# Weighted sums in 64-row halves of the array, projections in bursts, relu on two engines and squares on three

## The chip, the cores and the metric

The kernel runs on one core of one Trainium2 chip. A core has five engines that work side by side, each with its own queue of instructions in a fixed order: TensorE (PE in the profile; its weight loads are shown apart as PEld), VectorE (DVE), ScalarE (ACT), GpSimd (POOL) and SyncE (SP), which here only issues transfers. TensorE writes its results to a small memory, PSUM, in eight banks; VectorE and ScalarE read them there and write to the large on-chip memory. The metric is the device time of one execution, in microseconds (us).

## The reference

Two operators follow one another. The first is a gated attention without softmax, the second a gate with a long convolution along the sequence. For 8 batches, a sequence of S = 3136 and a width of D = 256 (`z` has a width of 64):

```
scores = z @ z.T / S                       # 3136 x 3136, per batch
attn   = maximum(scores, 0) ** 2
x      = u * (attn @ v)                    # 3136 x 256
x1, x2, x3 = split(x @ w_proj, 3)          # w_proj is 256 x 768
conv   = irfft(rfft(x2, axis=seq) * filter_fft, axis=seq)
out    = (x1 * conv * x3) @ w_out
```

The matrix `scores` is symmetric, so is `attn`.

## The kernel before

**Tiling.** A batch's columns of `attn` are cut into seven chunks (`CHUNKS`: five of 512, one of 256, one of 320), its rows into 25 tiles of 128, of which the last holds 64. For one chunk the kernel goes over the row tiles, two at a time (four in the 256-wide chunk); such a pair is a unit.
- *Scores* (`score_mm`, kind "S"): two matmuls with 64 rows of weights, because `z` is 64 wide. They lie in the upper and in the lower half of the array and run at the same time. Their two results fill a pair of PSUM banks; there are three such pairs (`ps_t`).
- *Relu* (line 1852) by ScalarE from PSUM to the buffer `R` in float32 (three of them), *square* (lines 1859 and 1861) by ScalarE or VectorE from `R` to `A` in bfloat16 (eight of them).
- *Weighted sum* (`weigh`, kind "W"): for each row tile and each of the two halves `dh` of the width one matmul with 128 rows, `v` as weights and `A` as the moving operand. All of a chunk add up in two PSUM banks, `ps_o[0]` and `ps_o[1]`. Some units, kind "M", need no scores: they take the transposed copy of a tile that was squared for an earlier chunk. The odd 64 rows at the end are added by `weigh_short`.
- *End of a chunk* (line 1903): VectorE multiplies the two finished banks with `u` and writes `x` (`xT`), two instructions for each bank; then the banks are free for the next chunk.
- *Projections and the convolution* (kinds "FA", "FB", "FZ", all with 128 rows): `x` times `w_proj`, the first and last steps of the Fourier transform, and the product with `w_out`. Their results go through single banks of the three pairs and leave by ScalarE or VectorE. The middle steps of the transform (`add_quads`, kind "Q") use quarters of the array, 64 rows by 64 columns.

**Shapes of the array.** So TensorE works in two shapes: with 128 rows (sums, projections) and with 64 rows (scores, quads; with 64 columns too while a quad is near, `plan.quarters`). All matmuls are issued by the helper at line 561, so the profile gives this line for all and tells them apart by tiles (`ps_s`, `ps_o_t`, `zT_t`, `v_t`).

**Order of the work.** Nothing loops on the chip: the class `Plan` writes out the order of every queue beforehand. It keeps a clock per engine, with a cost for each kind of work (`c_act`, `c_dve`, `c_pe`), and picks the next task of TensorE (`pick_pe`) and of the other engines (`pick`). A change between the two shapes is charged 0.096. While scores can start (a free pair of banks), they go on; else the plan turns to sums and projections. A table, `RULES`, gives the parameters of these choices for each 50 us of the plan's clock. Projections are let in by a credit: each sum adds `pace`, each projection takes its cost off; the credit goes no higher than 2.0. The plan only sets the order. On the chip each engine takes its queue in that order, and semaphores make it wait for what it needs.

**At the ends of a chunk** `add_weigh` puts the sums of the first and the last units for `dh = 1` off (`put_off`), so that the two banks begin and end at different times.

**Buffers and queues.** GpSimd issues the loads of `u`, `v` and `z` two chunks ahead; each such step begins with a copy of one element (`tick`, line 644), which waits for the chunk's `x`. SyncE issues the other transfers.

Of the kernel before, what the change touches and what calls it, by code (L numbers as in the profile page):

```python
# [12 lines left out]
P = 128  # L13
# [4 lines left out]
ALU = mybir.AluOpType  # L18
# [19 lines left out]
MOST = 3  # L38
REACH = 2
Rule = namedtuple("Rule", "backlog ample stay first lead pace full give")  # L40
STEP = 50.0
RULES = [
    Rule(1.25, 5.0, 0.05, 0.5, 1, 0.5, 3.0, 1.0),
    Rule(1.25, 5.0, 0.05, 0.5, 1, 0.5, 3.0, 1.0),
    Rule(1.25, 5.0, 0.05, 0.5, 1, 0.45, 3.0, 1.0),
    Rule(1.25, 5.0, 0.05, 0.5, 1, 0.45, 3.0, 1.0),
    Rule(1.25, 5.0, 0.05, 0.5, 1, 0.45, 3.0, 1.0),
    Rule(1.25, 5.0, 0.05, 0.5, 1, 0.5, 3.0, 1.0),
    Rule(1.25, 5.0, 0.05, 0, 1, 0.55, 3.0, 1.0),
    Rule(1.25, 5.0, 0.05, 0.5, 1, 0.5, 3.0, 1.0),  # L50
    Rule(1.25, 5.0, 0.05, 0.5, 1, 0.5, 3.0, 1.0),
    Rule(1.25, 6.0, 0.05, 0.5, 1, 0.5, 3.0, 1.0),
    Rule(1.25, 6.0, 0.05, 0.5, 1, 0.5, 3.0, 1.0),
    Rule(1.25, 5.0, 0.05, 0.5, 1, 0.5, 3.0, 1.0),
    Rule(0.5, 6.0, 0.05, 0, 0, 0.4, 99, 0.5),
    Rule(0.5, 6.0, 0.05, 0, 0, 0.4, 99, 0.5),
    Rule(0.5, 6.0, 0.05, 0, 0, 0.4, 99, 0.5),
    Rule(1.25, 5.0, 0.1, 1, 1, 0.5, 3.5, 1.0),
    Rule(1.75, 99.0, 0.3, 0.5, 1, 0.55, 4.0, 1.0),
    Rule(1.25, 5.0, 0.05, 0.5, 1, 0.5, 3.0, 0),  # L60
    Rule(1.25, 5.0, 0.3, 0.5, 1, 0.6, 3.0, 1.0),
    Rule(1.25, 5.0, 0.05, 0.5, 1, 0.5, 3.0, 0),
# [14 lines left out]
def c_dve2(n):  # L77
    return 0.068 + n * 0.00052

# [103 lines left out]
class Task:  # L183


    def __init__(self, emit, cost, deps=(), takes=(), prio=0, lat=None, moves=0.0, late=0.0):
# [6 lines left out]
        self.end = None  # L193
        self.holders = 1
# [11 lines left out]
class Plan:  # L206


    def __init__(self):
# [7 lines left out]
        self.soon = False  # L217
        self.n = 0
        self.spare = []
        self.pairs = None  # L220
        self.bus = 0.0

# [30 lines left out]
    def run(self, task, engine, start):  # L253
# [6 lines left out]
        task.end = end  # L260
        task.emit(engine)
# [36 lines left out]

    def pick_pe(self):
        t = self.free["PE"]  # L300
        now = self.rule(t)
        got = {}
        for k, window in (("S", 1), ("Q", 4), ("W", 1), ("FA", 6), ("FB", 6), ("FZ", 6)):
            best = None
            for task in self.queues[k][:window]:
                s = max(t, self.ready_at(task))
                if s < INF and (best is None or s < best[0] - 1e-9):
                    best = (s, task)
            if best:
                got[k] = best  # L310
        if not got:
            return None
        more = self.queues["S"]
        quad = got.pop("Q", None)
        if self.mode == "S" and self.quarters and quad and quad[0] <= t + now.stay:
            if not more or self.quad_run < 1 and self.score_run >= now.lead:
                return (*quad, "Q")
        if more and not more[0].left:
            left = self.backlog()
            if self.mode == "S":  # L320
                if "S" in got and got["S"][0] <= t + now.stay:
                    return (*got["S"], "S")
                got.pop("S", None)
                if self.quarters and quad and quad[0] <= t + now.stay and self.quad_run < 1:
                    return (*quad, "Q")
            else:
                want = 3 if left > now.ample else 2
                free = self.pairs.when(min(want, len(more)) - 1)
                first = quad and quad[0] <= t + 0.3 and left > now.first
                if "S" in got and free > t + 0.04:  # L330
                    rest = {k: v for k, v in got.items() if k != "S" and (k == "W" or left > now.backlog)}
# [1665 lines left out]
```

## Time and profile before

| | |
|---|---|
| median of 3 runs | 986.96 us (986.27 to 987.56) |
| span of the profiled execution, first to last instruction | 983.6 us |
| TensorE busy | 946.7 us (96%), 6,776 matmuls |
| weight loads busy | 470.0 us (48%), 6,877 |
| VectorE busy | 832.4 us (85%) |
| ScalarE busy | 855.6 us (87%) |
| GpSimd busy | 204.4 us (21%) |
| granted TensorE clock, mean | 0.998 |

The page has no other time of the profiled execution than its span; what an execution takes before the first and after the last instruction is in the runs' times and not in it. How to read the rows: a row of a group names the line, the engine, the operation, what is written and read (tile names without buffer numbers), the shape, and after "x" the count; behind the bar stand the busy time in us, the mean duration of one in ns, and the idle time of the engine just before them with what ended it. "64\*128 64x512" is a matmul with 64 rows and 128 columns of weights and 512 columns of the moving operand. The busy time of TensorE is a union of matmul durations; as matmuls are pipelined, the distance from one start to the next tells more than a duration.

### The profile page before, as it was taken

To read this page: it belongs to the slowest core of one execution; us is meant where nothing else is said; L and a number is where in the kernel's file an instruction comes from. 1 tells how busy PE (TensorE), PEld (TensorE's weight loads), DVE (VectorE), ACT (ScalarE), POOL (GpSimd) and SP (SyncE) were. 2 spreads that over 40 slices of the span, in tenths; PEclk is the share of its full clock that TensorE was granted. 3 is DMA by queue.
4 is the path that set the end of the run, shared out by engine and by line. 5 is a ranking of instruction groups with operands and counts; after the bars stand their busy time and mean duration, and the time that the engine had idled before them with its cause. 6 is when DMAs were issued, how large, how long until landed. Compare 5 with 4: busy or idle time off the path is not lost.

```text
span 983.6 us, 19551 instructions
## 1 busy us (share of the span) xinstructions
PE 946.7 (96%) x6776; PEld 470.0 (48%) x6877; DVE 832.4 (85%) x1468; ACT 855.6 (87%) x1185; POOL 204.4 (21%) x426
## 2 busy tenths in 40 slices
PE   6999999999999999999999999999999999999986
PEld 2344544455544544445444454544544454544654
DVE  8966798998788887988879998799788997888885
ACT  5988898899888998899988899799988999999773
POOL 5142311222022301213111230113202222000040
PEclk9999999999999999999999999999999999999999
DMA  9799789979899689997699888997869978896677
GB/s 166 140 175 160 144 144 172 180 131 162 179 216 187 128 159 203 192 184 144 143 210 197 167 153 175 209 192 151 157 158 205 215 137 146 178 221 135 172 209 227
DMA packets 332403, 170.32 MB, mean 173 GB/s; under 512 B 242598, under 2 KB 307942, under 8 KB 332304
## 3 DMA queue, kind: packets, MB, share of 16 engines
q1 hardware_dynamic: 302496, 132.43, 63.1%
q0 software_dynamic: 29168, 35.13, 23.7%
q10 hardware_dynamic: 640, 1.51, 0.5%
q8 instruction: 54, 0.88, 0.4%
q14 instruction: 45, 0.37, 0.1%
HBM read 90.26 MB, written 53.35 MB: 146 GB/s over the span
## 4 chain that ended last, share of the span: by engine, by line
PE 77%; DVE 10%; ACT 5%; issue 5%; DMA 1%; ACTq 0%; POOL 0%; DVEq 0%; SPq 0%; POOLq 0%
PE ps_o_t L561 45%; PE ps_s L561 32%; DVE A_t L1861 4%; ACT R_t L1852 3%; DVE xT_t L1903 1%; DVE xh L1307 1%; DVE gate_t L1217 1%; DVE yT_t L1401 1%; ACT A_t L1859 1%; DMA spec<-s_t 0%; ACT x_t L594 0%; DVE gs_t L598 0%; ACT s_t L594 0%; DMA spec<-gs_t 0%; DMA zn_t<-in_z_dram 0%
## 5 line engine op out<-in xcount | busy, mean ns | idle before, releaser
L1852 ACT ACTIVATE R_t<-ps_s 128x1024 f32<-128x1024 f32 (+4 forms) x512 | 467.0, 965 | 71.2 <-PE ps_s L561 68.0
L561 PE MATMUL ps_o_t<-A_t,v_t 128*128 128x512 bf16 (+4 forms) x2009 | 447.5, 353 | 9.7 <-issue 4.8
L1861 DVE TENSOR_TENSOR A_t<-R_t 128x1024 bf16<-128x1024 f32 (+3 forms) x311 | 342.8, 1119 | 58.9 <-ACT R_t L1852 58.3
L561 PEld LDWEIGHTS <-v_t 128*128 128x128 bf16 (+2 forms) x2870 | 249.0, 98 | 259.8 <-issue 74.5
L1859 ACT ACTIVATE A_t<-R_t 128x1024 bf16<-128x1024 f32 (+4 forms) x185 | 186.5, 1018 | 1.2
L561 PE MATMUL ps_s<-zT_t 64*128 64x512 bf16 (+4 forms) x1512 | 169.9, 357 | 1.6 <-DVE zT_t L598 0.5
L644 POOL COPY tick<-xT_t 1x1 bf16<-1x1 bf16 x54 | 17.9, 331 | 693.7 <-DVE xT_t L1903 693.7
L561 PE MATMUL ps_s<-xT_t,wp 128*128 128x512 bf16 (+2 forms) x412 | 101.1, 351 | 3.6 <-ACT R_t L1852 0.9
L561 PEld LDWEIGHTS <-zT_t 64*64 64x64 bf16 (+1 forms) x1545 | 52.6, 101 | 101.7 <-issue 85.8
L594 ACT ACTIVATE x_t<-ps_s 128x512 bf16<-128x512 f32 (+2 forms) x152 | 82.2, 583 | 16.0 <-PE ps_s L561 12.1
L1903 DVE SCALAR_TENSOR_TENSOR xT_t<-ps_o_t,uT_t 128x256 bf16<-128x256 f32 (+2 forms) x224 | 76.1, 383 | 10.8 <-PE ps_o_t L561 8.6
L1307 DVE TENSOR_TENSOR xh<-xh,H 128x1024 bf16<-128x1024 bf16 x120 | 82.3, 686 | 0.8
L561 PE MATMUL ps_o_t<-M_t,v_t 128*128 128x512 bf16 (+2 forms) x352 | 81.8, 353 | 0.0
L1217 DVE TENSOR_TENSOR gate_t<-ps_s,x_t 128x256 bf16<-128x256 f32 (+2 forms) x214 | 71.0, 384 | 12.5 <-PE ps_s L561 10.7
L1401 DVE TENSOR_TENSOR yT_t<-ps_s,gate_t 128x512 bf16<-128x512 f32 (+2 forms) x98 | 58.4, 626 | 11.1 <-PE ps_s L561 10.1
L561 PEld LDWEIGHTS <-wp 128*128 128x128 bf16 x448 | 42.6, 98 | 45.6 <-issue 10.3
L635 POOL DMA_DIRECT2D un_t<-in_u_dram x112 | 60.1, 561 | 5.3 <-issue 4.5
L654 POOL DMA_DIRECT2D v_t<-in_v_dram x112 | 59.6, 557 | 4.8 <-DMA v_t<-in_v_dram 1.9
L598 DVE CAST xh<-ps_s 128x512 bf16<-128x512 f32 x62 | 41.8, 687 | 18.6 <-PE ps_s L561 17.7
L561 PE MATMUL ps_s<-wp,xT_t 128*128 128x256 bf16 x398 | 56.6, 273 | 0.2
L561 PE MATMUL ps_s<-wo,yT_t 128*128 128x256 bf16 (+1 forms) x338 | 49.8, 273 | 0.7 <-ACT R_t L1852 0.4
L594 ACT ACTIVATE s_t<-ps_s 128x512 bf16<-128x512 f32 (+1 forms) x82 | 46.9, 593 | 1.8 <-issue 0.9
(165 smaller groups left out, 840.9 us busy)
## 6 DMA issues: line engine op xcount, KB each, us to landing
out_dram<-ost_t SPq DMA_DIRECT2D x60, 256.0 KB
spec<-s_t SPq DMA_DIRECT2D x96, 128.0 KB
spec_in_t<-spec SPq DMA_DIRECT2D x56, 192.0 KB
spec<-gs_t SPq DMA_DIRECT2D x56, 192.0 KB
v_t<-in_v_dram POOLq DMA_DIRECT2D x80, 128.0 KB, 4.8
un_t<-in_u_dram POOLq DMA_DIRECT2D x80, 128.0 KB, 5.4
conv_in_t<-spec SPq DMA_DIRECT2D x34, 256.0 KB
out_dram<-ost_t SPq DMA_DIRECT2D x18, 128.0 KB
```

The lines of the kernel that those rows point to most:

```text
L561: wrote(nc.tensor.matmul(o, *args, **kw), o)
L594: got = nc.scalar.activation(out_, in_, AF.Copy)
L598: got = nc.vector.tensor_copy(out_, in_)
L635: nc.gpsimd.dma_start(out=t[ds(j * N1, N1), lo - t0 : hi - t0, :], in_=x[:, n2 : n2 + hi - lo, :])
L654: nc.gpsimd.dma_start(out=t[ds(j * N1, N1), ds(v_at(a), (b - a) * D)], in_=r[:, n2 + a - lo : n2 + b - lo, :].rearrange("p t d -> p (t d)"),)
L1217: got = nc.vector.tensor_tensor(g[:, ::-1] if h == 0 else g, p, x, ALU.mult)
L1307: nc.vector.tensor_tensor(x[:, 1 - i], x[:, 0], h, ALU.mult)
L1401: got = nc.vector.tensor_tensor(yb["y"][:, dh, 0:w], p, gates[b, c, dh][:, 0:w], ALU.mult)
L1852: has_read(nc.scalar.activation(blocks(box["R"], n, cw)[:rows], p, AF.Relu), p)
L1859: nc.scalar.activation(a, r, AF.Square)
L1861: nc.vector.tensor_tensor(a, r, r, ALU.mult)
L1903: nc.vector.scalar_tensor_tensor(x, f, inv_s2, ut, ALU.mult, ALU.mult)
```

## The change

Six things are changed.
1. A unit's weighted sum can be split (`weigh_half`): if the array is in 64-row work when the plan picks it, each 128-row matmul is done as two 64-row ones. In the first phase rows 0 to 63 add into one of the two banks and rows 64 to 127 into the other; the second phase (a task of its own, kind "V", in the list `rest`) does it crosswise. `flip` says which way round. The two row halves must not write the same bank at once: where the rows that add into a bank change, `by_rows` puts an empty instruction on TensorE's queue that waits for the last matmul of the other rows. The plan charges 0.12 for it if nothing lies between.
2. `pick_pe` is written anew. Scores and sums alternate; second phases are gathered up to `many` before the rows are crossed. Projections start when the next sum waits for its banks (or the credit is above `lots`) and go on while there is credit, which may now rise to `cap` (mostly 4.0). All parameters in `RULES` are new.
3. The sums of the first and last units of a chunk aren't put off any more.
4. Relu may run on ScalarE or VectorE.
5. The square may run on ScalarE, VectorE or GpSimd. The plan lets VectorE's squares, VectorE's products with the filter and GpSimd's squares follow one another and not overlap (`ports`), and gives GpSimd one only where it would be done sooner there than on both others.
6. Single banks: up to six may be in use at once (`MOST`, before three). Two loads of the last batch wait for the transform of the batch before (`after_q`).

```diff
-MOST = 3
+MOST = 6
...
+def c_pool(n):
+    return 0.25 + n * 0.0021
...
     def pick_pe(self):
...
+        runs = [k for k in ("S", "Q") if k in got and got[k][0] <= t + now.stay]
...
+        if self.rest:
+            if self.apart or self.flip in (None, self.rest[0].flip):
+                return max(t, self.ready_at(self.rest[0])), self.rest[0], "V"
+            if w and len(self.rest) < now.many:
+                return (*w, "W")
+            if runs:
+                return (*got[runs[0]], runs[0])
+            later = min(((*got[x], x) for x in ("S", "Q") if x in got), key=lambda x: x[0], default=None)
+            if later and later[0] <= t + now.hold:
+                return later
+            return max(t, self.ready_at(self.rest[0])), self.rest[0], "V"
+        kinds = ("FB", "FA", "FZ")
+        fs = [k for k in kinds if k in got and got[k][0] <= near]
+        if self.phase:
+            if fs and (self.credit > 0 or blocked or not self.queues["S"]):
+                return (*got[fs[0]], fs[0])
...
+            self.phase = False
+        if (blocked or self.credit > now.lots) and (fs or self.owed(t)):
...
+            if fs:
+                self.phase = True
+                return (*got[fs[0]], fs[0])
+        if w and self.score_run >= now.lead:
+            if self.mode != "S" or self.pairs.when() <= t + now.many * w[1].cost["PE"] / 2 + now.hold:
+                return (*w, "W")
+        if runs:
+            return (*got[runs[0]], runs[0])
+        if w:
+            return (*w, "W")
+        order = ["S", "Q", "W", "FA", "FB", "FZ"]
         k = min(got, key=lambda k: (got[k][0], order.index(k)))
         return (*got[k], k)
...
+            if e == "POOL" and others:
+                end = s + task.cost[e] - self.rule(t).slack
+                if any(end >= self.could_end(task, o, s) for o in others):
+                    continue
...
-                half = k in ("S", "Q")
+                half = k in ("S", "Q", "V") or k == "W" and self.mode == "S"
...
+                        if self.flip not in (None, task.flip) and not self.apart:
+                            start += 0.12
...
+                    task.split = half and task.second is not None
+                    if task.split:
+                        task.cost["PE"] /= 2
+                        task.second.flip = task.flip ^ 1
+                        self.rest.append(task.second)
...
+    def by_rows(dh, h, *args, **kw):
+        other, last = row_sums.get(dh, (h, None))
+        if other != h:
+            tc.add_manual_dep(
+                nc.tensor.nop().ins, last.ins.name, mybir.DependencyInfo(needs, reason.DATA),
+                reason="the other rows' sum",
+            )
+        inst = nc.tensor.matmul(*args, **kw)
+        row_sums[dh] = h, inst
...
+    def weigh_half(un, flip, first):
...
+            for h in range(2):
+                dh = h ^ flip
+                at = slice(h * N1, (h + 1) * N1)
...
+                for m in range(0, P, N1 if plan.quarters else P):
+                    p = N1 if plan.quarters else P
+                    by_rows(
+                        dh, h, o[ds(m, p)], row(v16[b], t)[at, ds(dh * P + m, p)], x,
+                        start=k == 0 and i == 0 and first, stop=last and i == len(pair) - 1 and not first,
+                    )
...
-        k, n = un[2], global_k
-        if k in (0, n - 3, n - 2):
-            part((0,))
-            if k in (0, n - 3):
-                put_off.clear()
-            put_off.append(part)
-            return None
-        if k in (1, n - 1):
-            part((0,))
-            for late in put_off:
-                late((1,))
-            return part((1,))
         return part((0, 1))
...
-                has_read(nc.scalar.activation(blocks(box["R"], n, cw)[:rows], p, AF.Relu), p)
+                if e == "ACT":
+                    has_read(nc.scalar.activation(r, p, AF.Relu), p)
+                else:
+                    has_read(nc.vector.tensor_single_scalar(r, p, 0.0, ALU.max), p)
...
-                    nc.vector.tensor_tensor(a, r, r, ALU.mult)
+                    (nc.vector if e == "DVE" else nc.gpsimd).tensor_tensor(a, r, r, ALU.mult)
...
-            r_ = on(
-                "ACT", relu, c_act(n * cw), [(st, -sum(costs[i + 1 :]) - extra)], [R_p.slots], prio=0
+            r_ = job(
+                None, relu, both(n * cw), [(st, -sum(costs[i + 1 :]) - extra)], [R_p.slots], prio=0
             )
-            how = {"DVE": c_dve(n * cw)} if (b, c) == (0, 0) and k > 1 else {"DVE": c_dve(n * cw), "ACT": c_act(n * cw) + 0.039}
+            how = {"ACT": c_act(n * cw) + 0.039, "DVE": c_dve(n * cw), "POOL": c_pool(n * cw)}
             q_ = job(None, sq, how, [r_], [a_p.slots], prio=1)
+            q_.ports = ("DVE", "POOL")
```

Of the new parameters, `many` is 2 in 14 of the 20 rows of `RULES`, 1 in four and 3 in two; `lots`, the credit from which projections start unasked, is 99 in 14, which is never, as `cap` is at most 6; `lead` is 1 in 16 and 2 in four.

235 lines of the change are left out of this document (146 added, 89 removed).

## The prediction

> **What bounds the kernel now.** I read the page first (busy shares, then the chain that ended last), then one window over the middle, then the table of waits, and last the timeline of TensorE around one change of array shape.
>
> ```profile
> span 983.6 us, 19551 instructions
> ...
> PE 946.7 (96%) x6776; PEld 470.0 (48%) x6877; DVE 832.4 (85%) x1468; ACT 855.6 (87%) x1185; POOL 204.4 (21%) x426
> ...
> PE 77%; DVE 10%; ACT 5%; issue 5%; DMA 1%; ACTq 0%; POOL 0%; DVEq 0%; SPq 0%; POOLq 0%
> ...
> 100.00:900.00 800.00, 787.14 (x5616) 389.17 (x5704) 689.11 (x1183) 719.33 (x988) 158.35 (x326) 1.00 0.89 173
> ...
> 400.00:500.00 100.00, 98.78 (x713) 48.66 (x723) 88.72 (x153) 92.32 (x129) 20.55 (x41) 1.00 0.89 164
> ...
> PEld L561 <- issue: 199.8, 559, 1.0
> ACT R_t L1852 <- PE ps_s L561: 68.0, 84, 4.2
> DVE A_t L1861 <- ACT R_t L1852: 58.3, 56, 2.4
> ```
>
> TensorE is busy 787 of the 800 us between 100 and 900 (columns of a window row: length, then PE, PEld, DVE, ACT, POOL, granted clock, DMA share, GB/s), at a granted clock of 1.00, and 77% of the last-ending chain is its own work. ScalarE's longest wait is for TensorE's scores (68.0 us), and VectorE's longest in this loop is for ScalarE's relu (58.3). So TensorE sets the pace, and the other two are close behind: 719.33 + 689.11 of 1,600 us is 88.0% over the middle, and the fullest stretch shown, 400 to 500, has 90.5% ((92.32 + 88.72)/200).
>
> But a busy TensorE isn't a streaming one, and the 559 idle spells of its weight loader that nothing but "issue" explains point at what is lost. The timeline shows one:
>
> ```profile
> 481.66 1.46 PE L561 MATMUL ps_o_t<-A_t,v_t 128*128 128x512 bf16 x6
> ...
> 483.05 0.33 PEld L561 LDWEIGHTS <-zT_t 64*128 64x128 bf16 x6 [0.42 <-issue]
> 483.05 0.82 PE L561 MATMUL ps_s<-zT_t 64*128 64x512 bf16 x6
> 483.55 1.96 ACT L1852 ACTIVATE R_t<-ps_s 128x1024 f32<-128x1024 f32 x2
> ...
> 483.81 1.47 PE L561 MATMUL ps_o_t<-A_t,v_t 128*128 128x512 bf16 x6
> ...
> 5.94 1.03 PE L561 MATMUL ps_s<-zT_t 64*128 64x512 bf16 x4 [0.52 <-DVE zT_t L598]
> ...
> 956.86 0.30 PE L561 MATMUL ps_s<-R_t,zT_t 64*64 64x256 bf16 x4
> ...
> L561 PE MATMUL ps_o_t<-A_t,v_t 128*128 128x512 bf16 x1389 | 357.8, 381 | 9.5 <-issue 4.8 <-DVE A_t L1861 1.3 <-DVE xT_t L1903 0.2
> ...
> L561 PE MATMUL ps_s<-zT_t 64*128 64x512 bf16 x487 | 74.2, 383 | 0.8 <-DVE zT_t L598 0.5
> ...
> L561 PEld LDWEIGHTS <-zT_t 64*128 64x128 bf16 x616 | 22.6, 94 | 53.1 <-issue 43.7 <-DVE xT_t L598 0.8 <-DVE zT_t L598 0.8
> ```
>
> Six 128-row matmuls take 1.46 us with 0.38 for the last alone, so they follow one another every (1.46 - 0.38)/5 = 0.216 us. The six that start at 481.66 should be followed at 481.66 + 6 x 0.216 = 482.96. The scores start at 483.05, 0.09 late. They are six matmuls on 64 rows, which run two at a time: 3 x 0.216 = 0.65, so the next weighted sum could start at 483.70; it starts at 483.81, 0.11 late. One stay in the half array costs 483.81 - 481.66 - 9 x 0.216 = 0.206 us more than the work. Read through the whole timeline, the array changes from 128-row to 64-row work 261 times (the rows at 5.94 and 956.86 are in the first and the last); 2 x 261 = 522 changes make up most of the 559 "issue" spells. **261 x 0.206 = 53.8 us**, 5.5% of the span, is what changes of shape cost now.
>
> **The change part by part.** (a) *Weighted sums in row halves.* While the array is in 64-row work, a task of four 128-row matmuls becomes eight 64-row ones: rows 0 to 63 add into one half of the output, rows 64 to 127 into the other, at once; a second phase crosses them. Two 64-row matmuls pass in the 0.216 us that one 128-row matmul takes (scores above), and two weight loads of 94 ns each fit in it even one after the other, so the streaming time stays as it is. Score, sum, score, sum can follow without a change of shape, and only projections still need the full array.
>
> (b) *Projections in longer bursts.* A burst begins when the head of the sums' queue waits for its output banks, that is once per chunk, and lasts while credit (now capped at 4.0 us) is left. There are 56 chunks (the row below: four products per chunk and one semaphore wait each). The largest projection groups are busy 101.1 + 56.6 + 49.8 = 207.5 us, 3.7 us per chunk, so one burst per chunk can hold them all.
>
> ```profile
> L1903 DVE SCALAR_TENSOR_TENSOR xT_t<-ps_o_t,uT_t 128x256 bf16<-128x256 f32 (+2 forms) x224 | 76.1, 383 | 10.8 <-PE ps_o_t L561 8.6
> ...
> L1903 DVEq EVENT_SEMAPHORE  x56: 21/368/2069, 28.5 to 924.1; - x56
> ...
> L561 PE MATMUL ps_s<-xT_t,wp 128*128 128x512 bf16 (+2 forms) x412 | 101.1, 351 | 3.6 <-ACT R_t L1852 0.9
> ...
> L561 PE MATMUL ps_s<-wp,xT_t 128*128 128x256 bf16 x398 | 56.6, 273 | 0.2
> ...
> L561 PE MATMUL ps_s<-wo,yT_t 128*128 128x256 bf16 (+1 forms) x338 | 49.8, 273 | 0.7 <-ACT R_t L1852 0.4
> ```
>
> The floor is 56 stays, the ceiling 261 as now. Against the floor speaks the last line of the picking rule: when no score, quad or sum is ready, a ready projection is taken wherever it stands. I take one of these per chunk (56 more) and 8 for head and tail: 120 stays, 120 x 0.206 = **24.7 us**. Bounds: 11.5 and 53.8.
>
> (c) *The price of a flip.* Between the phases TensorE must wait until the other rows' last matmul into the same bank is done; this is a new wait on its own work, and everything behind it on its queue waits too. No row shows it. From below it is nothing: work that is put between hides it. From above: a matmul of this form lasts 0.383 us, and the first reader of a score starts 0.12 us after it (483.05 + 0.38 = 483.43 against 483.55), so the next could start 0.383 + 0.12 after the last instead of 0.216: 0.29 us. The nearest row is the change of shape, 0.09. With one score pair (0.216) in between 0.07 is left, with two nothing. The program has about 640 sum tasks (24 row tiles x 2 output halves x 56 chunks = 2,688 matmuls, four or, in the 256-wide chunk, eight to a task), most rules gather two before they flip, and scores number 512 (the relu row below), so there is usually a score for each flip: 320 flips, half of them with one score between, 160 x 0.07 = **11.2 us**. Bounds: 0 and 320 x 0.29 = 93.
>
> (d) *The chunk's end.* So far one output half was finished ahead of the other (the put-off parts), which hid the products that empty it. Now both end together, and the next chunk's sums wait for four products of 0.383 us, 1.5 us. The projection burst of 3.7 us hides it; if none were ready it would cost up to 56 x 1.5 = 86 us, but scores are there as well. Zero taken. A squared tile is held until the second phase, up to two sums (1.7 us) longer, with eight buffers: zero. Up to six instead of three single banks may be held by projections, so a score after a burst may find no free pair for one evacuation: zero taken, up to 0.69 us (a 512-column cast, below) x 56 = 38 from above. The added order on the last batch's loads concerns SyncE, 0% of the chain: zero.
>
> (e) *Relu on two engines, squares on three.*
>
> ```profile
> L1852 ACT ACTIVATE R_t<-ps_s 128x1024 f32<-128x1024 f32 (+4 forms) x512 | 467.0, 965 | 71.2 <-PE ps_s L561 68.0
> ...
> L1852 ACT ACTIVATE R_t<-ps_s 128x1024 f32<-128x1024 f32 x408 | 402.5, 1038 | 62.7 <-PE ps_s L561 59.9 <-DVE A_t L1861 1.2
> ...
> L1861 DVE TENSOR_TENSOR A_t<-R_t 128x1024 bf16<-128x1024 f32 x238 | 287.3, 1220 | 46.8 <-ACT R_t L1852 46.3
> ...
> L1859 ACT ACTIVATE A_t<-R_t 128x1024 bf16<-128x1024 f32 x154 | 164.6, 1080 | 1.0
> ...
> L598 DVE CAST xh<-ps_s 128x512 bf16<-128x512 f32 x62 | 41.8, 687 | 18.6 <-PE ps_s L561 17.7
> ...
> L644 POOL COPY tick<-xT_t 1x1 bf16<-1x1 bf16 x54 | 17.9, 331 | 693.7 <-DVE xT_t L1903 693.7
> ```
>
> A relu on VectorE has no row; a cast of half its size takes 0.687, so it lies between 1.22 (VectorE's square of that size) and 1.37, against 1.04 on ScalarE: swaps, no saving. A square on GpSimd has no row either: not below 1.22, and its only row here is a one-element copy, 0.33. What counts is the relief of ScalarE and VectorE. They do 1,408 us in the middle 800. If this becomes 776 us (see the sum), they need 1,408/1,552 = 90.7%, just what 400 to 500 reaches. Fifty squares on GpSimd would take off some 57 us (1.08 to 1.22 each): 87%. So I put (e) at nothing on the path. A GpSimd square ahead of a load's issue delays it by one square; loads are asked for two chunks (2 x 983.6/56 = 35 us) ahead.
>
> The Trainium skill, "GPSIMD Engine Reference", section "Performance versus the Vector engine", has tensor_tensor 1.96 times slower there than on VectorE; an estimate by it is 1.96 x 1.22 = 2.39 us a square, which no run here shows yet. By it the sum stays the same, since such a square is given only where nobody waits.
>
> **Sum** on the profiled execution: 983.6 - 53.8 + 24.7 + 11.2 = 965.7 us. The median of the runs shown, 986.96, is 3.4 us above the span, the time around the first and last instruction. Forecast: **969 us**, 1.8% faster.
>
> **The rivals.**
> *Flips decide* (slower). The gain before flips is 53.8 - 24.7 = 29.1 us; with 320 flips it is gone at 0.09 us each, the price of a change of shape now. For it: the wait stands in TensorE's own queue, so nothing behind it, weight loads included, is sent early. Against it: scores can lie between. At 0.15 each: 983.6 - 29.1 + 48 + 3.4 = 1,006 us. Beside it: the Trainium skill, "TensorEngine Tiling (Array Packing)", "Gotcha 1: PSUM Pressure", says that different row tiles cannot use the same PSUM bank at once and software must keep them apart; this is why the wait cannot be dropped.
>
> *ScalarE and VectorE set the end.* Long bursts leave them short of work and the score stretches overload them. If they don't get beyond today's 88.0% and GpSimd takes only ten squares, nothing but 11/0.88/2 = 6 us is gained: 981 us. For it: 68.0 and 58.3 us of waits on TensorE show that they run dry already. Against it: 90.5% is reached over 100 us.
>
> *GpSimd holds VectorE up* (slower). VectorE's squares, 343 us over all forms, and GpSimd's read the same tile memory. Blocked time loads VectorE beyond what squares on GpSimd take off it. With 100 squares there (115 us off), blocked for t each, the two engines need 1,408 - 115 + 100 t in the middle, at 90.5% of two: the middle stays at 800 us or over from t = 1.55 (1,448/1.81 = 800); that is where it decides. At 1.8 it is 1,473/1.81 = 814, so 987 + 14 = 1,001 us. For it: nothing here shows the two together. Against it: the plan keeps them apart in its own time. Beside it: the Trainium skill, "SBUF — State Buffer", "Who interferes with whom", says that a VectorE instruction with two SBUF inputs and a GpSimd one that reads SBUF exclude each other for a whole instruction.
>
> *All goes well.* 70 stays (14.4 us), flips hidden: 983.6 - 53.8 + 14.4 + 3.4 = 947.6.
>
> *Sums stay whole.* A sum is split only if the array is in 64-row work when it is picked. If most were picked right after bursts, the shape would change as often as now: 987. Against it: scores come first after a burst.
>
> **How the numbers follow.** The forecast's own case (955 to 978) has 0.48; all goes well 0.15; ScalarE and VectorE set the end 0.15 (of it 0.09 faster, 0.03 the same, 0.03 slower); flips 0.13; GpSimd 0.07; sums whole 0.02 (the same). Faster by over 0.2%: 0.48 + 0.15 + 0.09 = 0.72; within 0.2%, which is about what a measurement of this kernel can tell from no change: 0.05; slower: 0.23. The range 940 to 1,003 leaves out the better part of "all goes well" (0.07) and the worse halves of the two slower cases (0.10); alone, the likeliest case is 955 to 978.
>
> **What would show it.** (a) right: 64-row sums into the output tiles, every 0.216 us in pairs. (b) right: changes of shape near 240, and the loader's "issue" spells well below 559; wrong: still over 200 stays. (c): gaps before the first sum of a second phase, 0 to 0.07 us where scores lie between; wrong: 0.15 and more. (d) wrong: TensorE waiting at chunk ends for the products of line 1903. (e): GpSimd squares near or above 1.22 us, VectorE's squares still 1.22; wrong: VectorE's squares of two lengths. The forecast fails if TensorE's busy share in the middle falls below today's 98%: then an engine behind it has become the bound.

## The result, and the profile after

The changed kernel takes 1034.07 us (1032.11 to 1036.92) against 986.92 (986.27 to 987.56): 1.048 times as long (interval 1.046 to 1.050). Forecast was 969, range 940 to 1,003: wrong in direction and size. The profiled execution took 1035.53 us with a span of 1033.6, 50.0 above the span of before.

Busy shares and chain of the changed kernel's page, and two windows in the prediction's columns:

```profile
span 1033.6 us, 27106 instructions
...
PE 961.6 (93%) x10540; PEld 495.5 (48%) x10596; DVE 849.5 (82%) x1427; ACT 846.4 (82%) x1189; POOL 266.8 (26%) x463
...
PE 39%; DVE 9%; ACT 4%; DMA 3%; issue 3%; SPq 1%; DVEq 0%; ACTq 0%
```

```profile
100.00:900.00 800.00, 762.52 (x8608) 393.34 (x8649) 670.13 (x1090) 679.80 (x944) 200.77 (x340) 0.99 0.86 161
400.00:500.00 100.00, 96.05 (x1027) 50.05 (x1026) 88.85 (x140) 87.02 (x120) 24.86 (x44) 1.00 0.89 174
```

TensorE is busy 762.52 of the middle 800 us (95.3%; before 787.14, 98.4%). This is the sign the prediction had named for its failure: something behind TensorE has become the bound. But ScalarE and VectorE are less busy too, (679.80 + 670.13)/1,600 = 84.4% against 88.0%. All three wait more, and the rows below show that much of it is for each other. The table of waits (time in all, times, longest) shows where:

```profile
PEld L631 <- issue: 124.3, 306, 3.7
PEld L1790 <- PE ps_o_t L1790: 103.2, 281, 0.6
DVE xT_t L2022 <- PE ps_o_t L1790: 45.3, 18, 5.0
...
PE ps_s L631 <- ACT R_t L1968: 9.0, 17, 1.2
...
PE ps_s L631 <- DVE R_t L1970: 8.8, 9, 3.5
```

The loader's "issue" spells, which stood for changes of shape, fell from 559 to 306, as forecast. New is that the loader waits 281 times for TensorE's own last sum (the flips), and that VectorE stands 45.3 us at the product that empties a finished sum (8.6 us before), 2.5 us each time, with its other work queued behind.

To size this I followed TensorE's matmuls through both traces from start to start and counted what each came later than streaming allows (0.216 us for 512 columns, the prediction's rows; less for fewer columns in proportion). A few per cent of the matmul records are missing from the traces, so the counts are close and not exact:

```
us of TensorE's time                       before    after
changes of array shape                       50.1     18.6   (522 and 180 changes, and 13 between two 64-row forms)
wait for its own other rows (flips)           0       23.1   (133 places)
waits over 0.3 us that VectorE ends           8.7     35.8
waits over 0.3 us that ScalarE ends           7.1     18.4
at half the clock                             0        8.3
short waits and all else                                     (+11.7)
stretches of projections, whole run         243.8    265.9   (334 and 99 stretches)
scores, sums, transforms, whole run         727.6    755.2
```

So the saving on shape came (31.5 us), flips took 23.1 of it, and 38.4 us are new waits for ScalarE and VectorE. Seen by place, projections in long bursts take 22.1 us more, the scores and sums 27.6 more in spite of the saving.

### The profile page after: what moved, and what is told of

Read it like the earlier page. It is cut to its first block, busy times and chain, and to the rows that moved or that the text cites. A ratio compares the mean times of both kernels' runs of the same rounds, so it can differ in the third digit from the quotient of the medians.

```text
span 1033.6 us, 27106 instructions
## 1 busy us (share of the span) xinstructions
PE 961.6 (93%) x10540; PEld 495.5 (48%) x10596; DVE 849.5 (82%) x1427; ACT 846.4 (82%) x1189; POOL 266.8 (26%) x463
## 4 chain that ended last, share of the span: by engine, by line
PE 39%; DVE 9%; ACT 4%; DMA 3%; issue 3%; SPq 1%; DVEq 0%; ACTq 0%
PE ps_o_t L1790 19%; PE ps_s L631 18%; PE ps_o_t L631 3%; DVE xh L1379 2%; ACT R_t L1968 2%; DMA spec_in_t<-spec 1%; DVE A_t L1979 1%; DMA M_t<-A_t 1%; DVE yT_t L1476 1%; DVE xh L1384 1%; DVE xh L668 1%; ACT A_t L1977 1%; DVE gate_t L1287 1%; DVE xh L1383 0%; DVE R_t L1970 0%
## 5 line engine op out<-in xcount | busy, mean ns | idle before, releaser
L1790 PE MATMUL ps_o_t<-A_t,v_t 64*64 64x512 bf16 (+5 forms) x4860 | 459.7, 358 | 5.4 <-issue 0.8
L1968 ACT ACTIVATE R_t<-ps_s 128x1024 f32<-128x1024 f32 (+4 forms) x385 | 358.2, 960 | 46.6 <-PE ps_s L631 34.5
L1790 PEld LDWEIGHTS <-v_t 64*128 64x128 bf16 (+1 forms) x6406 | 232.8, 100 | 254.4 <-PE ps_o_t L1790 103.2
L1979 DVE TENSOR_TENSOR A_t<-R_t 128x1024 bf16<-128x1024 f32 (+2 forms) x219 | 241.7, 1134 | 41.3 <-ACT R_t L1968 19.7
L1977 ACT ACTIVATE A_t<-R_t 128x1024 bf16<-128x1024 f32 (+3 forms) x240 | 232.2, 985 | 43.5 <-DMA M_t<-A_t 15.6
L631 PE MATMUL ps_s<-zT_t 64*128 64x512 bf16 (+5 forms) x1346 | 195.6, 357 | 13.8 <-DVE R_t L1970 7.7
L1970 DVE TENSOR_SCALAR R_t<-ps_s 128x1024 f32<-128x1024 f32 (+3 forms) x127 | 140.5, 1129 | 29.1 <-PE ps_s L631 20.1
L1979 POOL TENSOR_TENSOR A_t<-R_t 128x1024 bf16<-128x1024 f32 (+3 forms) x37 | 68.8, 1863 | 251.2 <-ACT R_t L1968 133.9
L2022 DVE SCALAR_TENSOR_TENSOR xT_t<-ps_o_t,uT_t 128x256 bf16<-128x256 f32 (+2 forms) x224 | 71.3, 381 | 46.4 <-PE ps_o_t L1790 45.3
L631 PEld LDWEIGHTS <-zT_t 64*128 64x128 bf16 (+1 forms) x1379 | 65.3, 99 | 83.2 <-issue 40.4
L1790 PE MATMUL ps_o_t<-M_t,v_t 64*64 64x512 bf16 (+4 forms) x932 | 91.2, 360 | 0.7 <-DMA M_t<-A_t 0.3
```

What stands on the lines that cost most here:

```text
L631: wrote(nc.tensor.matmul(o, *args, **kw), o)
L1790: inst = nc.tensor.matmul(*args, **kw)
L1968: has_read(nc.scalar.activation(r, p, AF.Relu), p)
L1970: has_read(nc.vector.tensor_single_scalar(r, p, 0.0, ALU.max), p)
L1977: nc.scalar.activation(a, r, AF.Square)
L1979: (nc.vector if e == "DVE" else nc.gpsimd).tensor_tensor(a, r, r, ALU.mult)
```

## The experiments

Each run was timed on the same chip as a set of runs of before, whose medians lie between 986.77 and 987.37 us. All ratios are to the kernel before; the accounts of TensorE's time are counted as above.

**1. Flips and GpSimd's squares, taken out of the changed kernel's own order.** Same rows in both phases:

```diff
-                dh = h ^ flip
+                dh = h
```

> The changed kernel in its own order, but the second phase of a split sum does the same rows into the same banks again instead of crossing them, so no wait between rows is left (half of each split sum's products are done twice and the other half left out). Flips as a main cost (24 us of starts held back for the other rows, by the trace of the changed kernel): 1,034 falls by 20 to 30 us, to 1,004 to 1,014. Flips hidden, the loss lying with ScalarE, VectorE and GpSimd: it falls by under 8 us, since what TensorE gains it waits for the squares.

GpSimd's 37 squares made light:

```diff
-                    (nc.vector if e == "DVE" else nc.gpsimd).tensor_tensor(a, r, r, ALU.mult)
+                    if e == "DVE":
+                        nc.vector.tensor_tensor(a, r, r, ALU.mult)
+                    else:
+                        nc.gpsimd.tensor_copy(a[:, 0, 0:1], r[:, 0, 0:1])
+                        nc.gpsimd.memset(A[:rows, 1 : n * cw], 0.0)
```

> The changed kernel in its own order, but each of GpSimd's 37 squares is a copy of one column, which keeps the wait for its relu, and a fill of the rest, which reads nothing (these 37 squares are left out). GpSimd holding VectorE's reads up: VectorE's product with the filter and its sums go back to 0.69 and 0.42 us, and the time falls by 5 to 15 us, the 3 us stall of TensorE near 764 us gone. GpSimd harmless: within 3 us of the changed kernel.

Both:

> Both edits at once, same order. If flips and GpSimd's squares are all that the new order loses on the chip: 987 to 1,000 us. If TensorE's waits for ScalarE and VectorE come from the order itself: above 1,005.

Measured: same rows 1024.83 us, ratio 1.038 (1.036 to 1.040), between what its two theories gave; light squares 1021.62, 1.036 (1.033 to 1.039); both 1009.49, 1.023 (1.020 to 1.027). Flips are worth 9 us alone and 12 on top of the light squares, though TensorE's own wait of 23.1 us is gone: waits that VectorE and ScalarE end rose from 54.2 to 64.5 us with same rows, so they were next. GpSimd's squares are worth 12.5 us. Squares, and VectorE's products and sums in the transforms, in the changed kernel and then with light squares (groups by shape; after the count busy time and mean ns of one):

```profile
L1979 DVE TENSOR_TENSOR A_t<-R_t 128x1024 bf16<-128x1024 f32 x174 | 207.3, 1222 | 29.8 <-ACT R_t L1968 16.3 <-PE ps_o_t L1790 7.8 <-DMA M_t<-A_t 3.4
...
L1379 DVE TENSOR_TENSOR xh<-xh,H 128x1024 bf16<-128x1024 bf16 x120 | 85.3, 718 | 2.3 <-ACT xh L664 0.2
...
L1979 POOL TENSOR_TENSOR A_t<-R_t 128x1024 bf16<-128x1024 f32 x29 | 58.4, 2018 | 188.7 <-ACT R_t L1968 116.1 <-issue 39.5 <-DVE R_t L1970 10.9
...
L1384 DVE TENSOR_TENSOR xh<-xh 128x512 bf16<-128x512 bf16 x56 | 31.9, 569 | 0.0
...
L1383 DVE TENSOR_TENSOR xh<-xh 128x512 bf16<-128x512 bf16 x56 | 30.1, 538 | 1.8
```

```profile
L1379 DVE TENSOR_TENSOR xh<-xh,H 128x1024 bf16<-128x1024 bf16 x120 | 81.4, 686 | 2.6 <-ACT xh L664 0.6
...
L1383 DVE TENSOR_TENSOR xh<-xh 128x512 bf16<-128x512 bf16 x56 | 23.8, 424 | 1.8
L1384 DVE TENSOR_TENSOR xh<-xh 128x512 bf16<-128x512 bf16 x56 | 23.4, 418 | 0.0
```

The sums go from 538 and 569 ns back to 424 and 418: GpSimd's squares had held them up. It isn't all sums that were slower: nine of the 112 took 2.00 to 2.12 us, the others at most 0.43. With both causes gone 22.7 us above before are still left, so neither alone, nor both, are the whole.

**2. Are row halves a gain at all?** The same order of work, but every split sum is done whole in the full array at its first phase's place:

```diff
-                "W", lambda: weigh_half(un, t.flip, True) if t.split else weigh(un, dhs), c_pe(*[cw] * (n * len(dhs))), deps,
+                "W", lambda: weigh(un, dhs), c_pe(*[cw] * (n * len(dhs))), deps,
...
-                    lambda e: weigh_half(un, t.flip ^ 1, False) if t.split else None, {"PE": c_pe(*[cw] * n)}, [(t, ISSUED)]
+                    lambda e: None, {"PE": c_pe(*[cw] * n)}, [(t, ISSUED)]
```

> The changed kernel in its own order, but every sum in whole 128-row matmuls at the place of its first phase, nothing at the place of the second. Row halves save what was forecast for them: 371 stays in the half array instead of 103, 268 x 0.206 = 55 us more for changes of shape, 24 us less for flips, so 1,034 + 31 = 1,065. Row halves worth nothing because TensorE waits for the others anyway: 1,030 to 1,045.

Measured 1067.32 us, 1.081 (1.079 to 1.084), 33.3 above the changed kernel. Its trace has 764 changes of shape that cost 73.7 us, 55.1 more than with row halves, and no flips, 23.1 less: 32.0. So the price of a change (73.7/764 = 0.096 us, 0.19 for two, where the prediction had 0.206) and that of the flips add up to what was measured, which they do only because what else differs between the two traces, other waits and the clock, nearly cancels. Row halves are a gain of 33 us in this order, and the loss is elsewhere.

**3. Part (e) alone, on the old order, and its two halves.** In the kernel before, relu on two engines and squares on three, planned anew by the old rules:

```diff
-            r_ = on(
-                "ACT", relu, c_act(n * cw), [(st, -sum(costs[i + 1 :]) - extra)], [R_p.slots], prio=0
+            r_ = job(
+                None, relu, both(n * cw), [(st, -sum(costs[i + 1 :]) - extra)], [R_p.slots], prio=0
...
-            how = {"DVE": c_dve(n * cw)} if (b, c) == (0, 0) and k > 1 else {"DVE": c_dve(n * cw), "ACT": c_act(n * cw) + 0.039}
+            how = {"ACT": c_act(n * cw) + 0.039, "DVE": c_dve(n * cw), "POOL": 0.25 + n * cw * 0.0021}
```

> The kernel before with one part of the change alone: relu on ScalarE or VectorE, squares on ScalarE, VectorE or GpSimd, sums and projections picked as before. If this part costs by itself, by GpSimd holding VectorE up and by a less regular order: 995 to 1,010 us. If it is the other parts' order that loses: within 5 us of before.

Only the relu (squares on two engines, without "POOL"):

> The order of before with the relu of a score on ScalarE or VectorE, squares on these two as before; nothing on GpSimd. Computes everything. Theory GpSimd (the squares on GpSimd, which hold VectorE up, are what part (e) costs): at most 0.5% from before, 984 to 992 us. Theory relu (a relu of 1.2 us on VectorE stands in front of the 0.4 to 0.7 us products that empty TensorE's banks, so these come late): 1,000 us or more, with TensorE waiting for VectorE at weighted sums and projections as it did with the whole of part (e), where stalls over 0.3 us on VectorE came to 34.9 us.

Only the squares (relu on ScalarE):

> The order of before with the squares on three engines, the relu on ScalarE alone. Computes everything. Theory GpSimd: most of what part (e) cost alone (33 us) comes back, 1,005 to 1,020 us. Theory relu: a few us, at most 63 squares x 0.3 us = 19 if each holds VectorE up as the 37 of the changed kernel did (12.5/37 = 0.34 us each), so 987 to 1,006 us.

Measured: both 1020.29 us, 1.034 (1.032 to 1.036), above the range expected; relu alone 994.04, 1.007 (1.005 to 1.009); squares alone 1012.39, 1.026 (1.021 to 1.031). So most of part (e)'s loss on the old order is GpSimd's squares, 25 us, as the GpSimd theory had it; relu on two engines costs 7, a little over the 992 us that this theory allowed it and short of the 1,000 of the other. The squares on two of the engines, and a wait, in the run with the squares alone on three engines (this profile is of the longest of its four executions, 1020.83 us):

```profile
L1861 DVE TENSOR_TENSOR A_t<-R_t 128x1024 bf16<-128x1024 f32 x167 | 216.8, 1303 | 62.9 <-ACT R_t L1852 55.4 <-issue 3.7 <-DMA out_dram<-ost_t 2.9
...
L1861 POOL TENSOR_TENSOR A_t<-R_t 128x1024 bf16<-128x1024 f32 x33 | 66.9, 2029 | 140.4 <-ACT R_t L1852 121.9 <-DMA conv_in_t<-spec 14.5 <-issue 4.0
```

```profile
ACT R_t L1852 <- POOL A_t L1861: 13.4, 6, 4.3
```

VectorE's mean square rises from 1220 to 1303 ns: 155 of the 167 keep at most 1.23 us, and twelve took 1.7 to 3.6. These are the squares of two lengths that the prediction named as the sign of its failure in (e). A second effect shows that I hadn't thought of: a 2.03 us square holds one of the three relu tiles, and ScalarE's next relu waited up to 4.3 us for such a square. The old rules do not keep GpSimd and VectorE apart as the changed plan does, so the two figures (25 and 12.5 us) are of different numbers of squares in different orders.

**4. The changed kernel without part (e), or without GpSimd.** The relu and square lines of before put back into the changed kernel; and in another run only "POOL" taken from the square's choices. Both are planned anew.

```diff
-            how = {"ACT": c_act(n * cw) + 0.039, "DVE": c_dve(n * cw), "POOL": c_pool(n * cw)}
+            how = {"ACT": c_act(n * cw) + 0.039, "DVE": c_dve(n * cw)}
-            q_.ports = ("DVE", "POOL")
```

> The changed kernel without part (e): row halves, two phases and bursts stay, relu on ScalarE alone, squares on ScalarE and VectorE. Computes everything. Theory part (e) (row halves and bursts are good by themselves, part (e) spoils them): after less the 33 us that part (e) cost alone, about 1,001 us; by the forecast's own terms 969 us. Theory bursts (long bursts and two phases leave ScalarE and VectorE short of work and then overload them, whatever the relu runs on): 1,020 us or more, with TensorE's waits over 0.3 us for these two at 50 us or more, as in the changed kernel (54.2).

> The changed kernel with squares on ScalarE and VectorE only, relu on both still; the order is planned for that. Computes everything. Theory GpSimd for the changed kernel: as with its 37 squares made one-column copies (1,021.6 us), 1,016 to 1,026 us. If the loss from GpSimd was particular to that order and no property of the squares: 1,030 us or more.

Measured 1027.81 us, 1.041 (1.037 to 1.044), and 1027.70, 1.040 (1.037 to 1.043). The theory that part (e) spoils a good order falls: it is worth only 6 us here (in orders that were planned anew and differ), and relu on two engines nothing. The second lies between what the two theories gave it; an order planned without GpSimd loses some of what light squares in the old one gain. Without part (e) TensorE's waits for the two engines are 39.3 us, so the 50 of the theory of bursts aren't reached either, but the time is the one that it gave, and projections take 264.0 us (before 243.8).

**5. Is it the load of VectorE and ScalarE?** The relu tile in bfloat16 makes VectorE's squares shorter, in both kernels:

```diff
-                box["R"] = R_p.tile()
+                box["R"] = R_p.tile([P, 2, 512], BF16)
```

> The changed kernel in its own order, but relu writes R in bfloat16 instead of float32, so VectorE's squares should take about 0.69 us (its product of two bfloat16 tiles of that size takes 0.69 before the change) instead of 1.22; a lighter load on VectorE without moving anything. If TensorE waits because VectorE and ScalarE are too slow for the bursts and the scores after them: its waits for them, 57 us in the middle, fall by half or more and the half-clock stretches go, 1,034 falls to 990 to 1,005. If it waits because of the order (one late step behind another, whatever they cost): under 12 us are gained.

> The kernel before in its own order, with the same edit. TensorE is busy 98% of the middle and waits there 13 us for the two engines, so VectorE's shorter squares can give back 5 to 13 us: 974 to 982. If VectorE was a bound as well: below 970.

Measured: the changed kernel 1027.45 us, 1.039 (1.035 to 1.043); before 983.37, **0.996 (0.995 to 0.998)**, the only version that leaves nothing out and beats both kernels (the relu is rounded to bfloat16 ahead of its square). VectorE's squares in this version of before:

```profile
L1861 DVE TENSOR_TENSOR A_t<-R_t 128x1024 bf16<-128x1024 bf16 x238 | 162.6, 687 | 88.4 <-ACT R_t L1852 82.2 <-DMA M2e_t<-A_t 3.6 <-DMA uT_t<-un_t 1.2
```

0.687 us instead of 1.220, 127 us of VectorE's time over these 238, bring 3.8 us, a little less than the 5 to 13 expected; in the changed kernel 6.6. VectorE is busy for 575 of the middle 800 us instead of 689, and in the changed kernel for 582 instead of 670. So VectorE's load isn't the main thing that TensorE waits for. No run makes ScalarE's instructions shorter, so the same isn't shown for ScalarE. I tried to go further and cut the squares of VectorE and GpSimd to a column and a fill:

```diff
+                    eng = nc.vector if e == "DVE" else nc.gpsimd
+                    eng.tensor_copy(a[:, 0, 0:1], r[:, 0, 0:1])
+                    eng.memset(A[:rows, 1 : n * cw], 0.0)
```

> The changed kernel in its own order of work; every square that is VectorE's or GpSimd's is left out but for its first column, the rest of its tile is set to zero (ScalarE's squares stay). Theory waits (TensorE is held up by VectorE and ScalarE, and its own order is better than before's but for the flips): of the 54 us of waits over 0.3 us for these two and the 8 us at half clock most go, 965 to 985 us. Theory TensorE (row halves and flips themselves take the time): little goes, above 1,005 us.

> As the one before, and in addition the second phase isn't crossed, so that no sum waits for the other rows (half of the split sums' products are made twice, the other half left out). With the other waits gone, the difference of the two is what flips cost TensorE when nothing else holds it: by the wait for other rows counted in the changed kernel's trace 23 us (which the run with same rows alone didn't return, 9 us), by the forecast's term 11 us. Theory waits: 945 to 965 us. Theory TensorE: above 990 us.

> The kernel before in its own order; VectorE's squares are left out but for their first column, the rest of the tile set to zero. The yardstick for the two others: the trace of before has 16 us of waits over 0.3 us for VectorE and ScalarE and 9 us of shorter ones, so 960 to 980 us. By theory waits the changed kernel's light version is at or below this one, by at most 31.5 - 23 = 8 us; by theory TensorE it is 30 us or more above it.

Measured 1016.69 us, 1.030 (1.026 to 1.034); with same rows 1004.53, 1.017 (1.012 to 1.022); before made light 984.48, 0.997 (0.995 to 0.998). The edit takes off less than was meant. The changed kernel's fill:

```profile
L1981 DVE MEMSET A_t<- 128x1023 bf16 x174 | 158.5, 911 | 27.7 <-issue 23.1 <-DVE A_t L1980 4.0 <-PE ps_o_t L1790 0.3
L1980 DVE CAST A_t<-R_t 128x1 bf16<-128x1 f32 x219 | 29.1, 133 | 46.4 <-ACT R_t L1968 28.1 <-DMA M_t<-A_t 9.7 <-PE ps_o_t L1790 7.4
```

0.911 + 0.133 is no light square against 1.22, so these runs don't reach "no load". The changed kernel's two times lie where the theory of TensorE had them (above 1,005 and above 990) and over 30 us above those of the theory of waits; but with so little taken off this doesn't decide between the two, and before made light stayed above the 960 to 980 expected too. What the runs give: flips are worth 12 us here too, as in experiment 1, and in the shortest of these versions of the changed kernel (1004.53) projections still take 260.4 us, 17 above before, while scores, sums and transforms take 727.9, just before's 727.6.

**6. Bursts alone, on the old order.** No row halves, no part (e); a burst starts at more credit, lasts longer and may hold six banks. And six banks with nothing else (`MOST = 6`):

```diff
-MOST = 3
+MOST = 6
...
+        self.phase = self.credit > (-1 if self.phase else 2)
+        fs = [k for k in ("FA", "FB", "FZ") if k in got and got[k][0] <= t + 0.2]
+        if self.phase and fs and self.mode != "S":
+            k = min(fs, key=lambda k: got[k][0])
+            return (*got[k], k)
...
-        order += ["FA", "FB", "W", "FZ"] if self.credit > 0 and self.queued(t) < now.full else ["W", "FA", "FB", "FZ"]
+        order += ["FA", "FB", "W", "FZ"] if self.phase and self.queued(t) < now.full else ["W", "FA", "FB", "FZ"]
...
-                    self.credit = min(self.credit + self.rule(start).pace, 2.0)
+                    self.credit = min(self.credit + self.rule(start).pace, 4)
```

> The order of before with the rule of the bursts alone changed: a burst of projections starts at a credit of 2.0 us, lasts while any is ready within 0.2 us and the credit is above -1, and may hold six single banks. No row halves, no part (e). Computes everything. Theory bursts (steps of projections one right behind the other wait for each other's results on ScalarE and VectorE): slower, 1,000 to 1,030 us, with TensorE's waits over 0.3 us at projections well above the 7 us of before. Theory of the forecast (bursts cost nothing by themselves): within 1% of before, 977 to 997 us.

> The kernel before with six single banks instead of three for projections and nothing else. Computes everything. Theory bursts: within 1% of before, 980 to 997 us, since bursts stay 0.6 us long. If the banks that projections hold keep scores waiting, as the forecast's upper bound of 38 us had it: 1,000 us or more.

Measured 1014.41 us, 1.028 (1.024 to 1.032), and 988.88, 1.002 (1.001 to 1.004). Longer bursts by this rule, with neither row halves nor part (e), cost 27 us; six banks almost nothing. Between 20 and 900 us a burst streams 0.59 us on average before, 0.87 in this run (the longest 5.0) and 2.36 in the changed kernel (5.6). TensorE's waits at sums and projections in the run with longer bursts, then the same in before:

```profile
PE ps_o_t L566 <- DVE A_t L1866: 6.2, 12, 0.9
...
PE ps_s L566 <- ACT x_t L599: 3.4, 7, 1.1
```

```profile
PE ps_o_t L561 <- DVE A_t L1861: 1.3, 4, 0.4
...
PE ps_s L561 <- ACT x_t L594: 0.7, 2, 0.5
```

Projections wait for casts and the sums for squares, both more than before. TensorE's waits over 0.3 us that VectorE and ScalarE end come to about 20 us more in this trace than in that of before; they are most of the 27. Of the 28.4 us that the stretches take longer, 6.4 lie in projections and 22.0 in scores, sums and transforms. My expectation looked for them at projections alone.

## Why the prediction was wrong

*(a) The price of a change of shape: right.* 180 changes and 13 smaller ones cost 18.6 us, forecast 240 and 24.7; experiment 2 confirms the price by putting the changes back. 64-row sums stream in pairs at 0.216 us, as the changed kernel's timeline shows:

```profile
488.13 0.59 PE L1790 MATMUL ps_o_t<-A_t,v_t 64*128 64x512 bf16 x4
...
488.57 0.38 PE L631 MATMUL ps_s<-zT_t 64*128 64x512 bf16 x2
...
488.80 0.61 PE L1790 MATMUL ps_o_t<-M_t,v_t 64*128 64x512 bf16 x4
...
612.46 4.35 PE L1790 MATMUL ps_o_t<-A_t,v_t 64*128 64x512 bf16 x32
...
613.56 0.55 PEld L1790 LDWEIGHTS <-v_t 64*128 64x128 bf16 x8 [0.56 <-PE ps_o_t L1790]
614.66 0.55 PEld L1790 LDWEIGHTS <-v_t 64*128 64x128 bf16 x8 [0.56 <-PE ps_o_t L1790]
615.76 0.55 PEld L1790 LDWEIGHTS <-v_t 64*128 64x128 bf16 x8 [0.56 <-PE ps_o_t L1790]
```

Two pairs from 488.13 to 488.57 are 0.22 each; a score; and the next sums 0.23 after it.

*(c) Flips: the size.* With a score of 512 columns between, the next phase comes 0.01 to 0.02 us late (488.57 to 488.80), less than the 0.07 taken. But the sum let every flip have one score or two before it, and that failed: 78 flips stand directly behind the other rows' sums, with nothing in between. The row at 612.46 holds 16 pairs, and the weight loader shows three such flips in it: 4.35 - 15 x 0.216 - 0.38 = 0.73, so 0.24 each, within the bound of 0.29 and more than a whole stay (0.206). All 78 make 18.2 of the 23.1 us, 0.23 each. Taken out, flips returned 9 to 12 us; that this is near the 11.2 of the sum is luck, since other waits took over. With the counted terms in place of the forecast's the sum is 983.6 - 50.1 + 18.6 + 23.1 + 3.4 = 979 us: still faster, so this term doesn't turn the sign.

*(b) and (d) Bursts: the steps that failed.* "One burst per chunk can hold them all" is true, 99 stretches of projections instead of 334, but it was costed at nothing. Experiment 6 puts the cost of a far milder lengthening of bursts, on the old order, at 27 us. The forecast asked whether scores find a free bank after a burst (38 us from above, zero taken). The run with six banks doesn't test this, as its bursts stay short (none streams over 2.2 us). The changed kernel's trace does: its scores' waits over 0.3 us for VectorE and ScalarE come to about 18 us, before's to 2, and some 13 of the 18 are for a relu that has yet to empty banks, the wait of the two rows on `R_t` in the table of waits. That term wasn't nothing. What the forecast didn't ask is whether the steps of a burst wait for each other: such waits at projections come to about 27 us (before 11), and in every version of the changed kernel projections took 12 to 33 us more than before's 243.8. Nor did it ask what the sums after a burst find. The wait that (d) looked for on TensorE, at chunk ends, stands on VectorE (45.3 us), with casts and relus that TensorE needs queued behind it. In the run without part (e) that wait is only 11.4 us and the time hardly better, so it is one form of the loss and not its cause:

```profile
DVE xT_t L2021 <- PE ps_o_t L1790: 11.4, 7, 2.9
```

*(e) "Nothing on the path": failed.* Part (e) alone on the old order costs 33 us, 25 of them by GpSimd's squares, and these 12.5 us in the changed kernel. The cover named, VectorE's and ScalarE's share falling to 87%, did come (84.4%), but a low share doesn't hide anything: the work that is held up is a link in a chain. (The 776 us from which the prediction worked out 90.7% and 87% isn't what its sum gives: 800 x 965.7/983.6 is 785 us, and the shares are then 89.7% and 86%.) A stretch of the changed kernel's timeline:

```profile
762.32 3.92 POOL L1979 TENSOR_TENSOR A_t<-R_t 128x1024 bf16<-128x1024 f32 x2 [10.97 <-ACT R_t L1968]
762.50 2.00 DVE L1383 TENSOR_TENSOR xh<-xh 128x512 bf16<-128x512 bf16 x1
...
764.42 2.11 DVE L1384 TENSOR_TENSOR xh<-xh 128x512 bf16<-128x512 bf16 x1
...
766.45 1.27 DVE L668 CAST xh<-ps_s 128x512 bf16<-128x512 f32 x2
...
767.18 1.01 PE L631 MATMUL ps_s<-wo,yT_t 128*128 128x256 bf16 x4 [2.89 <-DVE xh L668]
```

Two GpSimd squares make two VectorE sums of 0.42 us last 2.00 and 2.11, the cast behind them comes late, and TensorE stands for 2.89 us. The Trainium skill, "SBUF — State Buffer", section "Who interferes with whom", says that the one blocks the other for a whole instruction; these rows agree. (The prediction's sign for it, VectorE's squares of two lengths, all but failed to show in this kernel, where 173 of 174 kept at most 1.23 us and one took 1.64; it showed at these sums, and at the squares in the run of experiment 3 where only these are changed.) The rival on GpSimd had this mechanism, but set its threshold by VectorE's load (100 squares, blocked 1.55 us each). 37 squares were enough, since a late link costs at once. The plan keeps these instructions apart in its own time; on the chip nothing does.

*"ScalarE and VectorE set the end".* They do end TensorE's waits. For VectorE it isn't mainly its load, as experiment 5 shows with squares little more than half as long; for ScalarE that wasn't tested.

*What stays open.* With flips and GpSimd's squares out, 22.7 us above before remain, against a saving of 31.5 on shape: some 54 us that these two don't explain and that I put down to the order. In that run's trace projections take 13 us more than before, and scores, sums and transforms 9 more in spite of the saving. Bursts have such a cost by experiment 6; how much of the 54 is theirs and how much that of the two phases, which hold squared tiles and output banks longer, wasn't separated. No version with more than eight squared tiles was tried.

## What to carry to other kernels

Before a saving on the busiest engine is booked, look at what the new order asks of the engines behind it from one microsecond to the next: average busy shares of 84 to 88% on the engines behind didn't keep it from waiting here, because the steps depend on each other. Price work for an idle engine by the instructions that it can hold up and the buffers that it keeps. The wait between the two row halves was cheap here where a score of 512 columns stood between them (0.02 us) and dear where nothing did (0.23).

## What the runs showed of the hardware

- A 128x1024 square takes 2.02 us on GpSimd (the mean of 29; half of them took 1.88 to 1.89) and 1.22 on VectorE, 1.65 times; the estimate from the Trainium skill in the prediction was 2.39.
- A direct change of rows in a bank cost 0.23 to 0.24 us, more than going to 64-row work and back (0.19 to 0.21).
- After TensorE had stood, it ran at half clock for a while, five times before the last 10 us; in the 3.41 us before each it was busy for 0.5 to 2.2 us. Windows of the changed kernel, the seventh figure the granted clock:

```profile
109.00:119.00 10.00, 6.40 (x66) 3.36 (x62) 6.51 (x7) 4.61 (x6) 1.02 (x2) 0.83 0.73 136
...
764.00:772.00 8.00, 4.89 (x18) 2.16 (x18) 6.34 (x10) 3.79 (x7) 3.52 (x6) 0.63 0.81 156
```

In the second the half clock sets in during the 2.89 us wait above: the clock records show 0.5 for 6.83 us from 766.12. In the 3.41 us before it, from 762.71, TensorE was busy for 1.22 us. Such stretches cost 8.3 us by my count, a part of the loss that no step of the prediction had. The run without part (e) has none before 976 us and is 40.5 us above before all the same, so they are not the main loss. The Trainium skill, "TensorE: Matmul & The Clock Gate", "Part 1: The HAM clock gate", puts the return to half clock after at least one idle window of about 3.4 us; here it came although TensorE was busy for 1.22 of the 3.41 us before.
